# Decoding weights in the first batch's GEMM slots: the intermediate in PSUM, half of the low bits on GpSimd, two pieces ahead instead of four

## The chip, the core and the metric

The kernel runs on one core of one Trainium2 chip. The core has five engines that each work through their own instruction queue and meet only at semaphores: TensorE (PE in the profile, with PEld its weight loads), VectorE (DVE), ScalarE (ACT), GpSimd (POOL) and SyncE (SP), which here issues most of the DMAs. The metric is the device time of one execution in microseconds (us). Lower is better.

## The reference

Four batches, each in two stages: an mLSTM attention with gates (8 heads, 768 positions, head size 40), and a mixer that multiplies its output by two pairs of weight matrices.

```
for t in range(S):                                   # attention, per batch and head
    m_new = max(f[t] + m, i[t])
    C = exp(f[t] + m - m_new) * C + exp(i[t] - m_new) * outer(v[t], k[t])
    n = exp(f[t] + m - m_new) * n + exp(i[t] - m_new) * k[t]
    y[t] = sigmoid(o[t]) * (C @ q[t]) / max(|n . q[t]|, 1)
x = y as [4, 768, 320]
u = x + (relu(x.T @ w_tok1) @ w_tok2).T              # 768 -> 256 -> 768
out = u + relu(u @ w_ch1) @ w_ch2                    # 320 -> 1536 -> 320
```

The weights arrive as 64-bit floating-point numbers, so the kernel has to turn them into 32-bit ones itself before it can multiply by them.

## The kernel before

Attention works on chunks of 128 positions, a unit (b, c) being chunk c of batch b. The mixer of a batch consists of `a_part` and `a_end` (first pair, first product), `phase_b` (second product, added to x), `phase_t` (transposes of u, two blocks of 128 positions into one tile uT), and 18 GEMM slots. A slot (k, p) takes 256 positions k and 256 of the 1536 inner columns p: `gemm1` makes h in PSUM, ACT makes gh = relu(h) rounded, DVE makes gl = the remainder, and `gemm2`, which is issued one slot later, multiplies both by w_ch2. Every product is made of three matmuls, high by high, low by high and high by low half.

The first batch differs in that its weights are not there yet. They are decoded in 30 pieces of 128x384 numbers, 12 of them before the slots and the other 18 in slots 0 to 8, two in each; in order, two pieces of w_ch1 and two of w_ch2 in turn. The slots of this batch go (0,0), (1,0), (0,1), (1,1) and so on, so that two slots pass for each p. One piece goes through four engines:

- SP loads the raw 64-bit words into a tile wst (line 581).
- `dec_abs` (lines 587 to 598): ACT takes the upper word as a float, its absolute value times 2^-112, into a tile f (line 594), and puts the three top bits of the lower word into wst as an integer (line 595, "the low bits" below).
- `dec_ops` (lines 600 to 618): DVE shifts f left by three and ORs the low bits in (line 608, in place in f), then ORs the sign in (line 611) into the tile w.
- `dec_hi` (line 623): ACT rounds w to the high half c1h or c2h; `dec_low` (line 629): POOL subtracts for the low half c1l or c2l.

In the attention of the first batch (flag `early`) f lies in a PSUM bank of the pool ps_acc and is named pf in the profile. In the slots f lies in SBUF, is named wf, and f and w are the same tile.

PSUM has eight banks in four pools of two. The pool ps_s (tag "s") holds the attention's scores, and in the first batch's slots the outputs of `phase_t` and of `phase_b` 4 and 5, each bank being handed to the next tile of that tag in the order of the code.

The order on every engine is the order of the code. In one slot n of the first batch up to n = 10 that is: `dec_ops` (DVE), `gemm1` with gh and gl, `dec_hi`, `dec_low`, `dec_abs` for the next pieces, a piece of sigmoid or of the next batch's preparation, then in slots 3 and 4 `phase_b` 4 and 5 (the list `extra`), then `gemm2` of the slot before.

Of the kernel before, what the change touches and what calls it, by code (L numbers as in the profile page):

```python
# [7 lines left out]
F32 = mybir.dt.float32  # L8
F32R = mybir.dt.float32r
I32 = mybir.dt.int32  # L10
U16 = mybir.dt.uint16
BF16 = mybir.dt.bfloat16
AF = mybir.ActivationFunctionType
ALU = mybir.AluOpType
# [16 lines left out]
W_BIAS = 2.0 ** -112  # L31
# [3 lines left out]
def kernel(ctx: ExitStack, tc: tile.TileContext, gates, qk, q3, kv, og,  # L35
                            wt1, wt2, wc1, wc2, ident, bmask, out):
    nc = tc.nc
# [5 lines left out]
    ps_acc = ctx.enter_context(tc.tile_pool(name="ps_acc", bufs=2, space=PSUM))  # L43
    ps_s = ctx.enter_context(tc.tile_pool(name="ps_s", bufs=2, space=PSUM))
    ps_m = ctx.enter_context(tc.tile_pool(name="ps_m", bufs=2, space=PSUM))

    def f32(x):
        return x.bitcast(F32)
# [8 lines left out]
    wq = tc.alloc_tile_pool(name="wq", bufs=1, side="right")  # L57
# [46 lines left out]
    floor_b = wp.tile([128, 1], F32, name="floor_b")  # L104
# [24 lines left out]
    def cols_w(c0, c1):  # L129
        n = c1 - c0  # L130
        t = ps_m.tile([128, n, B * HP], F32, tag="m", name="gw")
        e = id_t[0:B * HP, 0:B * HP]
        for i in range(n):
            a, z = (c0 + i) * L, (c0 + i + 1) * L
            nc.tensor.matmul(t[:, i], b_t[:, a:z], e, start=True, stop=False)
            nc.tensor.matmul(t[:, i], phi[:, z - 1:z].to_broadcast([B * HP, 128]), e, start=False, stop=True)
        return t
# [427 lines left out]
    WP = 384  # L565
# [6 lines left out]
    staged, ready = {}, {}  # L572
    nxt = [0, 0, 0]
    his, lows, wx, early = [], [], [], [True]
# [12 lines left out]
    def dec_abs(n):  # L587
        while nxt[1] < min(n, len(pieces)):
            raw = staged[nxt[1]]
            if early[0]:  # L590
                f = ps_acc.tile([128, WP], F32, tag="acc", name="pf")
            else:
                f = wq.tile([128, WP], F32, tag="wf", name="wf", bufs=4)
            nc.scalar.activation(f, raw[:, :, 1].bitcast(F32), AF.Abs, scale=W_BIAS)  # L594
            nc.scalar.activation(raw[:, :, 0], raw.rearrange("p n t -> p (n t)").bitcast(U16).rearrange("p (n t) -> p n t", t=4)[:, :, 1],  # L595
                                 AF.Identity, scale=2.0 ** -13, bias=floor_b)
            ready[nxt[1]] = (f, wq.tile([128, WP], F32, tag="wf", name="wf", bufs=4) if early[0] else f)
            nxt[1] += 1

    def dec_ops(more, m=2):  # L600
# [19 lines left out]
    def dec_hi():  # L620
        while his:
            _, _, f, d, _, a = his.pop(0)
            nc.scalar.activation(d[0][:, a:a + WP], f, AF.Copy)
            lows.append((f, d, a))

    def dec_low():
        while lows:
            f, d, a = lows.pop(0)
            nc.gpsimd.tensor_tensor(d[1][:, a:a + WP], f, f32(d[0][:, a:a + WP]), ALU.subtract)
# [9 lines left out]
    def a_part(b, j, s):  # L639
        _, xh, xl = xs[(b, s)]  # L640
        if s == 0:
            pa[j] = ps_h.tile([128, DM], F32, tag="h", name="ps_a")
        a = slice(s * DT + j * 128, s * DT + (j + 1) * 128)
        t = [(w1[0][:, a], xh), (w1[1][:, a], xh), (w1[0][:, a], xl)]
        mm3(pa[j], t, s == 0, s == NC - 1)
# [43 lines left out]
    acc = {}  # L689
# [16 lines left out]
    def gemm2(b, k, p, gh, gl, half=None):  # L706
        if p == 0 and half != 1:
            pool = (ps_m, "m") if (b, k) == (0, 1) else (ps_acc, "acc")
            acc[k] = [pool[0].tile([128, DM], F32, tag=pool[1], name=f"acc{i}") for i in range(2)]
        for tt in range(2) if half is None else (half,):  # L710
            t = slice(tt * 128, (tt + 1) * 128)
            a = [slice((2 * p + j) * DM, (2 * p + j + 1) * DM) for j in range(2)]
            mm3(acc[k][tt], [(gh[:, j, t], c2[x][:, a[j]]) for j in range(2) for x in range(2)]
                + [(gl[:, j, t], c2[0][:, a[j]]) for j in range(2)], p == 0, p == NF // 2 - 1)
            if p == NF // 2 - 1:
                s = 2 * k + tt
                x = xs[(b, s)][0]
                nc.vector.tensor_tensor(x, acc[k][tt], x, ALU.add)
                nc.sync.dma_start(out=out[b, s * 128:(s + 1) * 128, :], in_=x)


    def step(g, n=1):
        for _ in range(n):
            next(g, None)
# [37 lines left out]
    t = cols_w(0, 1)  # L762
# [12 lines left out]
    step(g, 9)  # L775
    split(1, 2)
    dec_abs(2)
    warm(10)
    spread_split(u1)
    t = cols_w(1, NC - 1)  # L780
# [88 lines left out]
    for b in range(B):  # L869
        if b:  # L870
            for j in range(2):
                for s in range(NC - 1):
                    a_part(b, j, s)
        if b == 1:
            step(ag)
        if b:
            gemm2(*pend, half=0)
        for j in range(2):
            a_part(b, j, NC - 1)
            a_end(b, j)  # L880
        if b:
            gemm2(*pend, half=1)
            pend = None
            phase_b(b, 0)
            phase_b(b, 1)
            if b < B - 1:
                phase_b(b, 2)
                phase_t(b, 0, ss)
                phase_t(b, 1, ss)
                step(ag, 2)  # L890
                phase_b(b, 3)
            else:
                phase_t(b, 0, ss)
                phase_b(b, 2)
                phase_t(b, 1, ss)
                phase_b(b, 3)
                step(ag)
        if b:
            slots = [(k, p) for k in range(3) for p in range(6)]
        else:  # L900
            dec_hi()
            step(dg, 1)
            sp.release()
            wx += [tc.alloc_tile_pool(name="wx", bufs=1, side="right"), nxt[0]]
            dec_load(nxt[0] + 3)
            dec_hi()
            dec_low()
            pf = prep_first(units[NC], units[NC + 1])
            dec_abs(nxt[2] + 4)
            phase_b(b, 0)  # L910
            step(dg, 9)
            phase_b(b, 1)
            phase_t(b, 0, ss)
            phase_b(b, 2)
            phase_t(b, 1, ss)
            phase_b(b, 3)
            dec_hi()
            dec_low()
            slots = [(k, p) for p in range(6) for k in range(2)] + [(2, p) for p in range(6)]
        extra = []  # L920
        more = {1: [(phase_b, 4, ss)], 2: [(phase_t, 2, ss)], 4: [(phase_t, 3, ss)], 5: [(phase_b, 5)],
                9: [(phase_t, 4), (phase_t, 5, ss)]}
        for n, (k, p) in enumerate(slots):
            if b == 0 and n == 3:
                extra = [lambda: phase_b(0, 4, ss), lambda: phase_b(0, 5, ss)]
            if b == 0 and n == 1:
                gemm2(*pend)
                pend = None
            if b == 0 and n < 11:
                dg = dec_ops(9)  # L930
                step(dg, 4 if n == 0 else 9)
            g = gemm1(b, k, p)
            if b == 0 and n == 0:
                step(dg, 9)
            if b == 0:
                if n == 0:
                    phase_t(b, 2, ss)
                    phase_t(b, 3, ss)
                    warm(6, id_t.bitcast(BF16))
                if n == 11:  # L940
                    phase_t(0, 4, ss)
                    phase_t(0, 5, ss)
                    gemm2(*pend)
                    pend = None
                    wx[0].release()
                    wq.release()
                    xpool[1] = ctx.enter_context(tc.tile_pool(name="xp", bufs=1, side="right"))
                    step(ag)
                if n < 11:
                    dec_hi()  # L950
                    dec_low()
                    dec_abs(nxt[2] + 2)
                    if n < 6:
                        sigmoid(1, (n // 3,), slice(n % 3, n % 3 + 1))
                    if n in (0, 5, 7, 8, 9):
                        step(pf)
                elif n > 11:
                    o = STEPS0[n - 12]
                    step(ag, o[0])
                    gemm2(*pend, half=0)  # L960
                    step(ag, o[1])
                    gemm2(*pend, half=1)
                    pend = None
                    step(ag, o[2])
            else:
                for f, *a in more.get(n, ()):
                    f(b, *a)
                step(ag, STEPS[n])
            if extra:
                extra.pop(0)()  # L970
            if pend:
                gemm2(*pend)
            pend = (b, k, p) + g
# [56 lines left out]
```

## Time and profile before

| | us |
|---|---|
| median of 3 runs (lowest, highest) | 453.13 (451.94, 453.14) |
| the profiled execution | 453.32 |
| its span, first to last instruction | 451.5 |
| mean granted TensorE clock | 0.989 of full speed |

The span is 1.8 us shorter than the time of the same execution; what lies around it is launch and end. Times in the rows count from the span's start. The first batch's attention fills about 0 to 62 us, the steps before its slots 62 to 68.6, slots 0 to 11 from 68.6 to 117.6, and from there on the other batches' attention is interleaved with the slots.

A timeline row has the start, the duration, the engine, the line, the operation, the tiles as out<-in with their shapes, and how many instructions it sums; in brackets how long the engine had been idle and what ended it. A wait row has the engine and line, what it waited for, the sum, how often, and the longest. PEclk is the clock granted to TensorE in parts of full speed: 1.00 is 2.4 GHz and 0.50 is 1.2 GHz.

### The profile page before, as it was taken

The numbers are of one execution on the slowest core, as the hardware profiler recorded it, in microseconds if no ns is written. First come the engines' busy times: TensorE is split into PE (matmuls) and PEld (weight loads), VectorE is DVE, ScalarE is ACT, GpSimd is POOL, SyncE is SP. The second block draws the span as 40 slices with busy tenths as digits, with TensorE's granted clock in tenths as the row PEclk, the third lists the DMA queues.
The fourth block names the chain that finished last, engine by engine and source line by source line (L and its number), as shares of the span: only waits on it lengthen the run. The fifth ranks groups of instructions, "written<-read, shape, count | busy, mean of one in ns | idle before, by whom it ended". The sixth has DMA issues, their size and how long they took to land.

```text
span 451.5 us, 9377 instructions
## 1 busy us (share of the span) xinstructions
PE 434.0 (96%) x3717; PEld 413.8 (92%) x3718; DVE 304.9 (68%) x664; ACT 187.0 (41%) x429; POOL 126.1 (28%) x159
## 2 busy tenths in 40 slices
PE   6699989999999989999999999999999999999997
PEld 3478878999999989999999999999999999999996
DVE  6598968875567567879888578879887635232212
ACT  3437685988344462532341353441442212112111
POOL 4046642465045331034224212223314110000000
PEclk9899989999999989999999999999999999999999
DMA  8818875770276851313533621312631000000000
GB/s 223 277 42 265 247 232 194 233 225 19 97 217 198 242 181 63 132 43 95 165 111 120 205 70 50 134 47 78 176 105 43 1 2 29 1 1 29 1 30 29
DMA packets 24615, 52.55 MB, mean 116 GB/s; under 512 B 2556, under 2 KB 13364, under 8 KB 24572
## 3 DMA queue, kind: packets, MB, share of 16 engines
q1 hardware_dynamic: 24380, 51.78, 37.3%
q8 instruction: 29, 0.48, 0.5%
q10 hardware_dynamic: 192, 0.18, 0.1%
q14 instruction: 14, 0.11, 0.1%
HBM read 47.91 MB, written 4.04 MB: 115 GB/s over the span
## 4 chain that ended last, share of the span: by engine, by line
PE 77%; DVE 4%; ACT 2%; DMA 1%; issue 1%; POOL 1%; DVEq 0%; ACTq 0%; SPq 0%
PE ps_h L635 27%; PE acc L635 26%; PE ps_sc L280 4%; PE ps_a L635 4%; PE ps_b L635 4%; PE po L370 3%; PE po L396 2%; DVE wf L608 2%; PE pu L348 2%; PE po L375 2%; DMA wst<-in_wc_dram 1%; DVE wf L611 1%; PE po L340 1%; ACT wf L594 1%; ACT wst L595 1%
## 5 line engine op out<-in xcount | busy, mean ns | idle before, releaser
L635 PE MATMUL ps_h<-uT,c1h 128*128 128x256 f32 x720 | 140.3, 282 | 0.9 <-DVE uT L686 0.8
L702 ACT ACTIVATE gh<-ps_h 128x512 fp32r<-128x512 f32 x72 | 43.0, 597 | 180.1 <-PE ps_h L635 180.1
L635 PEld LDWEIGHTS ps_h<-uT,c1h 128*128 128x128 f32 x720 | 115.4, 188 | 2.0 <-DVE uT L686 1.0
L635 PE MATMUL ps_h<-uT,c1l 128*128 128x256 f32 x432 | 111.4, 280 | 0.0
L703 DVE SCALAR_TENSOR_TENSOR gl<-ps_h,gh 128x512 fp32r<-128x512 f32 x72 | 49.6, 689 | 82.4 <-ACT gh L702 82.1
L635 PE MATMUL acc<-c2h,gh 128*128 128x320 f32 x288 | 91.2, 324 | 0.0
L635 PE MATMUL acc<-c2l,gh 128*128 128x320 f32 x288 | 87.2, 311 | 0.0
L635 PEld LDWEIGHTS ps_h<-uT,c1l 128*128 128x128 f32 x432 | 81.4, 188 | 0.0
L635 PE MATMUL acc<-c2h,gl 128*128 128x320 f32 x288 | 66.4, 312 | 0.8 <-DVE gl L703 0.8
L635 PEld LDWEIGHTS acc<-c2h,gh 128*128 128x128 f32 x288 | 54.7, 190 | 1.3
L635 PEld LDWEIGHTS acc<-c2l,gh 128*128 128x128 f32 x288 | 54.8, 190 | 0.0
L635 PEld LDWEIGHTS acc<-c2h,gl 128*128 128x128 f32 x288 | 48.3, 189 | 1.9 <-DVE gl L703 1.8
L261 ACT ACTIVATE dd<-dd,bcol 128x128 f32<-128x128 f32 x144 | 45.8, 393 | 4.7 <-POOL dd L251 4.7
L415 POOL TENSOR_TENSOR sig<-sig,ht 128x320 f32<-128x320 f32 x18 | 14.8, 824 | 112.6 <-DVE ht L378 102.3
L290 DVE TENSOR_TENSOR dd<-ps_sc,dd 128x512 f32<-128x512 f32 x48 | 31.0, 681 | 3.0 <-PE ps_sc L280 2.9
L465 POOL TENSOR_TENSOR xl<-x,xh 128x320 fp32r<-128x320 f32 x18 | 15.8, 877 | 47.2 <-DVE xh L463 47.2
L280 PE MATMUL ps_sc<-raw 40*128 40x128 f32 x384 | 28.6, 285 | 0.0
L280 PEld LDWEIGHTS ps_sc<-raw 40*128 40x128 f32 x384 | 23.9, 187 | 3.7 <-issue 1.7
L396 PE MATMUL po<-kvt,dd 128*128 128x41 f32 (+1 forms) x192 | 23.6, 280 | 1.7 <-issue 1.7
L396 PEld LDWEIGHTS po<-kvt,dd 128*128 128x128 f32 x192 | 22.8, 194 | 1.9 <-issue 1.9
L251 POOL TENSOR_SCALAR_AFFINE_SELECT dd<-dd 128x1024 f32<-128x1024 f32 x18 | 22.9, 1273 | 3.7 <-DMA dd<-phi_d 1.9
L303 DVE TENSOR_TENSOR r<-dd 128x512 f32<-128x512 f32 x24 | 22.6, 979 | 0.0
(135 smaller groups left out, 760.6 us busy)
## 6 DMA issues: line engine op xcount, KB each, us to landing
dd<-phi_d SPq DMA_DIRECT2D x18, 512.0 KB
wst<-in_wc_dram SPq DMA_DIRECT2D x22, 384.0 KB
kvt<-in_kv_dram SPq DMA_DIRECT2D x24, 324.0 KB
raw<-in_qk_dram SPq DMA_DIRECT2D x48, 160.0 KB
sig<-in_og_dram SPq DMA_DIRECT2D x8, 480.0 KB
out_dram<-x SPq DMA_DIRECT2D x24, 160.0 KB
q3t<-in_q_dram SPq DMA_DIRECT2D x20, 180.0 KB
wst<-in_wt_dram SPq DMA_DIRECT2D x8, 384.0 KB
```

The lines of the kernel that those rows point to most:

```text
L251: nc.gpsimd.affine_select(dd, dd, pattern=[[0, H], [1, L]], compare_op=ALU.is_ge, fill=-1e30, base=0, channel_multiplier=-1)
L261: nc.scalar.activation(dd[:, h, :], dd[:, h, :], AF.Exp, bias=bcol[:, c, HP * b + h:HP * b + h + 1])
L280: nc.tensor.matmul(t["s"][hf][:, h, :], r[:, 1, h, :], r[:, 0, h, :], start=True, stop=True)
L290: nc.vector.tensor_tensor(dd, t["s"][hf], dd, ALU.mult)
L303: nc.vector.tensor_tensor(r[:, h], dd[:, h], top(dd)[:, h], ALU.subtract)
L370: nc.tensor.matmul(po[:, h - h0, 0:j1 - j0], p[i][:, ROW[h], :], w[:, h, j0:j1], start=h == h0 and i + j0 == 0, stop=c == 0 and h == h1 - ...
L396: nc.tensor.matmul(o, t["dd"][:, ROW[h], :], x, start=c == 0 and h == 0, stop=h == H - 1)
L415: nc.gpsimd.tensor_tensor(sg, sg, ht[:, :, 0:D], ALU.mult)
L465: nc.gpsimd.tensor_tensor(xl, x, f32(xh), ALU.subtract)
L635: nc.tensor.matmul(ps, a, m, start=(first and i == 0), stop=(last and i == n - 1))
L702: nc.scalar.activation(gh, ps, AF.Relu)
L703: nc.vector.scalar_tensor_tensor(gl, ps, 0.0, f32(gh), op0=ALU.max, op1=ALU.subtract)
```

## The change

Five edits in the decode of the slots. The tile f is a PSUM bank of ps_s in place of an SBUF tile, and w is always an SBUF tile of its own. Of the pieces in the slots every even one gets its low bits from GpSimd (a tensor_scalar, line 598 of the changed kernel), every odd one from ACT as before. The call of `dec_abs` ahead of slot 0 stands behind `phase_b` and `phase_t` in place of ahead of them, and it takes two pieces in place of four. `phase_b` 4 and 5 are issued ahead of `dec_abs` in slots 3 and 4 in place of behind the slot's other work. DMAs are issued in the same order.

```diff
     def dec_abs(n):
         while nxt[1] < min(n, len(pieces)):
             raw = staged[nxt[1]]
-            if early[0]:
-                f = ps_acc.tile([128, WP], F32, tag="acc", name="pf")
+            pool, tag = (ps_acc, "acc") if early[0] else (ps_s, "s")
+            f = pool.tile([128, WP], F32, tag=tag, name="pf")
+            nc.scalar.activation(f, raw[:, :, 1].bitcast(F32), AF.Abs, scale=W_BIAS)
+            low = raw[:, :, 0]
+            top16 = raw.rearrange("p n t -> p (n t)").bitcast(U16).rearrange("p (n t) -> p n t", t=4)[:, :, 1]
+            if early[0] or nxt[1] % 2:
+                nc.scalar.activation(low, top16, AF.Identity, scale=2.0 ** -13, bias=floor_b)
             else:
-                f = wq.tile([128, WP], F32, tag="wf", name="wf", bufs=4)
-            nc.scalar.activation(f, raw[:, :, 1].bitcast(F32), AF.Abs, scale=W_BIAS)
-            nc.scalar.activation(raw[:, :, 0], raw.rearrange("p n t -> p (n t)").bitcast(U16).rearrange("p (n t) -> p n t", t=4)[:, :, 1],
-                                 AF.Identity, scale=2.0 ** -13, bias=floor_b)
-            ready[nxt[1]] = (f, wq.tile([128, WP], F32, tag="wf", name="wf", bufs=4) if early[0] else f)
+                nc.gpsimd.tensor_scalar(low, top16, 2.0 ** -13, 2.0 ** -14 - 0.5, op0=ALU.mult, op1=ALU.add)
+            ready[nxt[1]] = (f, wq.tile([128, WP], F32, tag="wf", name="wf", bufs=4))
             nxt[1] += 1
@@ before slot 0
             pf = prep_first(units[NC], units[NC + 1])
-            dec_abs(nxt[2] + 4)
             phase_b(b, 0)
...
             dec_hi()
             dec_low()
+            dec_abs(nxt[2] + 2)
@@ in a slot
                     dec_hi()
                     dec_low()
+                    if extra:
+                        extra.pop(0)()
                     dec_abs(nxt[2] + 2)
...
-            if extra:
-                extra.pop(0)()
             if pend:
                 gemm2(*pend)
```

ACT's queue from the steps ahead of slot 0 to the first decode of slot 1, before (c2h and c1h are `dec_hi`, wf<-wst and wst<-wst the two halves of `dec_abs`, uT is `phase_t`):

```order
L623 ACTIVATE c2h<-wf 128x384 x2
L594 ACTIVATE wf<-wst 128x384
L595 ACTIVATE wst<-wst,floor_b 128x384
L594 ACTIVATE wf<-wst 128x384
L595 ACTIVATE wst<-wst,floor_b 128x384
L594 ACTIVATE wf<-wst 128x384
L595 ACTIVATE wst<-wst,floor_b 128x384
L594 ACTIVATE wf<-wst 128x384
L595 ACTIVATE wst<-wst,floor_b 128x384
L685 ACTIVATE uT<-ps_t 128x3x128 x2
L702 ACTIVATE gh<-ps_h_929 128x512
```

and of the changed kernel, whose line numbers are two higher from line 599 on:

```order
L625 ACTIVATE c2h<-wf 128x384 x2
L687 ACTIVATE uT<-ps_t 128x3x128 x2
L592 ACTIVATE pf<-wst 128x384 x2
L596 ACTIVATE wst<-wst,floor_b 128x384
L704 ACTIVATE gh<-ps_h_925 128x512
```

Eight decode instructions stood ahead of the uT copies; three now stand behind them.

POOL's queue through the low halves of slots 0 to 3 in the changed kernel; before, the L631 rows (L629 there) stood next to each other:

```order
L631 TENSOR_TENSOR c1l<-wf,c1h 128x384 x2
L598 TENSOR_SCALAR wst<-wst 128x384
L631 TENSOR_TENSOR c2l<-wf,c2h 128x384 x2
L598 TENSOR_SCALAR wst<-wst 128x384
L631 TENSOR_TENSOR c1l<-wf,c1h 128x384 x2
L598 TENSOR_SCALAR wst<-wst 128x384
L631 TENSOR_TENSOR c2l<-wf,c2h 128x384 x2
```

Each new instruction stands behind the two subtractions of the slot before the one whose piece it serves.

PE's queue in slot 3, with waits, before (ps_b is `phase_b` 4, acc the `gemm2` of slot 2):

```order
L635 MATMUL ps_h_1108<-uT,c1l 128x256
L635 MATMUL ps_b<-rh,w2h 128x320
L635 MATMUL ps_b<-rh,w2l 128x320
L635 MATMUL ps_b<-rh,w2h 128x320
L635 MATMUL ps_b<-rh,w2l 128x320
```

and now:

```order
L637 MATMUL ps_h_1116<-uT,c1l 128x256
L637 MATMUL ps_b<-rh,w2h 128x320 [waits DVE_49]
L637 MATMUL ps_b<-rh,w2l 128x320
L637 MATMUL ps_b<-rh,w2h 128x320
L637 MATMUL ps_b<-rh,w2l 128x320
```

The order is the same; the first matmul of `phase_b` 4 now waits for DVE, whose line 611 (613 now) of slot 3's first piece is the last reader of the bank it writes. That of `phase_b` 5 in slot 4 has the same new wait.

## Rows read from the trace of the kernel before

**Rows 1.** The page: busy time, share of span and instructions of each engine.
```profile
PE 434.0 (96%) x3717; PEld 413.8 (92%) x3718; DVE 304.9 (68%) x664; ACT 187.0 (41%) x429; POOL 126.1 (28%) x159
```

**Rows 2.** Waits of PE, 55 to 112: us in total, times, longest.
```profile
PE ps_a L635 <- ACT xh L446: 1.4, 1, 1.4
PE acc L635 <- DVE gl L703: 0.8, 3, 0.4
PE ps_h L635 <- DVE uT L686: 0.8, 1, 0.8
```

**Rows 3.** Timeline of DVE, slots 0 to 8: start, us, what, [idle before].
```profile
71.12 1.02 DVE L608 SCALAR_TENSOR_TENSOR wf<-wf,wst 128x384 int32<-128x384 int32 x2
72.06 1.02 DVE L611 SCALAR_TENSOR_TENSOR wf<-wst,wf 128x384 int32<-128x384 int32 x2
85.15 1.02 DVE L611 SCALAR_TENSOR_TENSOR wf<-wst,wf 128x384 int32<-128x384 int32 x2
87.83 1.53 DVE L608 SCALAR_TENSOR_TENSOR wf<-wf,wst 128x384 int32<-128x384 int32 x2 [0.37 <-ACT wst L595]
106.52 1.02 DVE L611 SCALAR_TENSOR_TENSOR wf<-wst,wf 128x384 int32<-128x384 int32 x2
```

**Rows 4.** Timeline of PE in the slots, and after its longest later wait.
```profile
82.45 0.30 PE L635 MATMUL ps_b<-rh,w2h 128*128 128x320 f32 x1
86.98 0.31 PE L635 MATMUL ps_b<-rh,w2h 128*128 128x320 f32 x1
108.20 0.56 PE L635 MATMUL acc<-c2h,gl 128*128 128x320 f32 x2 [0.20 <-DVE gl L703]
163.34 2.46 PE L396 MATMUL po<-kvt,dd 128*128 128x41 f32 x16 [1.74 <-issue]
```

**Rows 5.** Timeline of ACT between two decode steps.
```profile
85.74 1.00 ACT L623 ACTIVATE c2h<-wf 128x384 fp32r<-128x384 f32 x2 [0.31 <-DVE wf L611]
87.09 0.66 ACT L595 ACTIVATE wst<-wst,floor_b 128x384 int32<-128x384 uint16 x1
87.62 0.56 ACT L594 ACTIVATE wf<-wst 128x384 f32<-128x384 f32 x1
88.06 0.65 ACT L595 ACTIVATE wst<-wst,floor_b 128x384 int32<-128x384 uint16 x1
```

**Rows 6.** Timeline of POOL, the low halves of slots 0 and 3.
```profile
73.81 2.00 POOL L629 TENSOR_TENSOR c1l<-wf,c1h 128x384 fp32r<-128x384 f32 x2 [8.66 <-ACT c1h L623]
86.34 2.01 POOL L629 TENSOR_TENSOR c2l<-wf,c2h 128x384 fp32r<-128x384 f32 x2 [2.11 <-ACT c2h L623]
```

**Rows 7.** Waits of DVE, 68 to 112.
```profile
DVE wf L608 <- POOL c1l L629: 2.1, 2, 1.0
DVE wf L608 <- POOL c2l L629: 2.1, 2, 1.0
```

**Rows 8.** Timeline around the first slot, ACT and PE.
```profile
67.73 0.86 ACT L685 ACTIVATE uT<-ps_t 128x384 fp32r<-128x384 f32 x2
70.14 0.71 PE L635 MATMUL ps_h<-uT,c1h 128*128 128x256 f32 x3 [0.77 <-DVE uT L686]
```

**Rows 9.** Groups of POOL by form: busy, mean ns, idle before.
```profile
L629 POOL TENSOR_TENSOR c2l<-wf,c2h 128x384 fp32r<-128x384 f32 x10 | 10.0, 1023 | 12.0 <-ACT c2h L623 12.0
L102 POOL COPY sel<-id 128x360 bf16<-128x360 bf16 x1 | 0.5, 484 | 0.1
L92 POOL CAST late_b<-late 128x128 bf16<-128x128 f32 x1 | 0.3, 291 | 0.1
```

**Rows 10.** Timeline of DVE and POOL, attention stage: the intermediate pf in PSUM.
```profile
55.30 0.57 DVE L608 SCALAR_TENSOR_TENSOR pf<-pf,wst 128x384 int32<-128x384 int32 x1
54.86 1.04 POOL L629 TENSOR_TENSOR w2l<-wf,w2h 128x384 fp32r<-128x384 f32 x1
```

**Rows 11.** Windows: busy PE, PEld, DVE, ACT, POOL, then PEclk, DMA share, GB/s.
```profile
62.00:66.00 4.00, 3.86 (x15) 3.21 (x14) 2.50 (x7) 3.70 (x9) 1.99 (x2) 0.57 0.72 226
164.00:169.00 5.00, 5.00 (x27) 5.00 (x28) 2.83 (x8) 4.31 (x11) 1.91 (x3) 0.66 0.44 134
```

## The prediction

> **What bounds the kernel now.** I read the page first: PE is busy for 96% of the span [rows 1], so time is to be won or lost only where PE waits or runs at its lower clock. In PE's waits from the last attention unit of batch 0 to slot 10 the reader sees two small sums inside the changed stretch: 0.8 us for the transposed uT at slot 0 and 0.8 us, in three pieces, for the remainder gl in slots 6 to 8 [rows 2]. Then I followed what gl stands behind, DVE's timeline. In each slot DVE does the pair at line 608, the pair at line 611, then gl; the line-611 pairs begin at 72.06 in slot 0, 85.15 in slot 3, 106.52 in slot 8 [rows 3]. That is 34.46 us for eight rounds, 4.3 on average. DVE is far behind PE: slot 3's line-611 pair begins at 85.15, while PE has finished `gemm1` of slot 3 at 82.45 [rows 3, 4].
>
> The decode runs in a ring, here from slot 3 to slot 4. Line 611 begins at 85.15; ACT's rounding begins at 85.74, 0.59 later [rows 5]; POOL's subtractions begin at 86.34, 0.60 later, and take 2.01 [rows 6]; the ACT decode of the next pair is done at 88.06 + 0.65 = 88.71 [rows 5], yet DVE's line-608 pair, which began at 87.83 on the first piece, takes 1.53 in place of the 1.02 it takes when POOL is idle [rows 3]. It is held until POOL ends at 88.35. Waits of 4.2 us in total stand to POOL's name at this line [rows 7]. So the ring already closes on POOL's end, and PE begins to feel it in slot 6.
>
> **What each edit costs.** (1) `dec_abs` behind `phase_t`. Today ACT copies uT from 67.73, after eight decode instructions, and PE waits 0.77 at 70.14 for DVE's part [rows 8]. Without them the copies start as the transposes end; DVE's later work in that stretch moves forward by the same 0.8, so slot 0's line-611 pair begins near 71.3. PE gains little of it: its next work is `phase_t` 2, whose ps_s bank the line-611 instruction of slot 0's first piece must free first, 0.51 after 71.3 [rows 3]. That is about 71.9, where it starts today. I book nought for PE and minus 0.76 for the ring.
>
> (2) Low bits on POOL. ACT loses 87.62 - 87.09 = 0.53 per slot [rows 5], which the ring does not feel. POOL gets one instruction behind each pair of subtractions, and the first line 608 waits for its result. Its price P is shown by no row. From above, the subtraction of the same 384 elements, with two inputs, took 1.02; from below, a cast of 128 elements took 0.29. A one-input copy of 360 elements took 0.48, so 384 would take about 0.50 [rows 9]. It is the nearest, but its elements lie side by side and need no arithmetic, while here they are 8 bytes apart, with two operations and two conversions. I take 0.6.
>
> The Trainium skill (GPSIMD Engine Reference, section 7, Performance pitfalls for Q7 kernels) puts reads of up to 8 bytes step at about 1.9 cycles an element, and only wider steps at 2.9; at the 1.2 GHz of its section 1 that would be 384 x 1.9 / 1.2 = 0.61 us, an estimate from that page, before any start-up, and the sum below would be the same to 0.1. Its section 4.1 calls one-input work roughly line-rate, which at one element a cycle would be 0.32 and make the sum about 2 us smaller. No row here shows a strided read on POOL.
>
> (3) The intermediate in PSUM. Line 608 then runs beside POOL: in the attention stage, where f was in PSUM, it took 0.57 at 55.30 inside a subtraction that ran from 54.86 for 1.04 [rows 10]. So the hold of up to 0.5 per round goes, and the two line-608 instructions take 0.94 to the start of line 611 [rows 3]. But the round gains nothing from it, because DVE now waits for POOL by dependency, to the same POOL end and P beyond.
>
> The hand-over from POOL to DVE I take as 0.05, an estimate from the 0.08 between the end of the first line-611 instruction (85.15 + 0.51) and ACT's start. The new round: 0.59 + 0.60 + 2.01 + P + 0.05 + 0.94 = 4.19 + P, at P = 0.6 4.79, against 4.13 today from slot 3 to 4. Carried through: in slot 0 POOL's pair starts at 73.81 and takes 2.00 [rows 6], perhaps 0.15 later now; line 611 of slot 1 then begins at 73.96 + 2.00 + 0.6 + 0.05 + 0.94 = 77.55. Seven more rounds of 4.79 end at 111.1.
>
> (4) `phase_b` 4 in slot 3. Its bank is that of slot 3's first piece, so its first matmul waits for line 611 of slot 3, two rounds after 77.55, 87.1 + 0.55 = 87.7. PE is ready at about 82.45, as today [rows 4]. It waits about 5.2 us, with `gemm2` of slot 2 and `gemm1` of slot 4 queued behind it. Even with today's DVE times it would wait until 85.7, 3.2 us. What PE loses there it partly has back, since it then runs behind the ring and no longer waits in each slot. But from `phase_b` 4 to the end of `gemm1` in slot 4 PE needs 86.98 - 82.45 = 4.53 [rows 4], so slot 4's h is there at 92.2, and gh(4), 0.50 on ACT, stands ahead of that slot's rounding, which the ring would have wanted at 92.5. Rounding starts near 92.8: plus 0.3 on the ring. `phase_b` 5 then finds its bank nearly free.
>
> Sum on the ring: slot 8's line-611 pair begins at 111.1 + 0.3 = 111.4 against 106.52, plus 4.9. In slot 8 PE waits for gl both before and after [rows 4], so it passes on whole. Behind slot 8 nothing takes it back: the next batch's scores are issued on PE behind slot 11, and their loads wait on PE's and DVE's progress.
>
> (5) The clock. After PE's wait of 1.4 us at 59 to 61 [rows 2] the window 62 to 66 shows a granted clock of 0.57, most of it at 0.50, or 1.2 GHz; after the 1.74 before 163.34 [rows 4] the window 164 to 169 shows 0.66 [rows 11]. The loss is 4 x 0.43 = 1.7 and 5 x 0.34 = 1.7 us of work. A wait of 5.2 us is longer than both, and the work behind it up to gh(4) is on the ring; I book 1.5, since a part of the slow stretch may fall into the wait.
>
> Total: 4.9 + 1.5 = 6.4 on the profiled execution's 453.32, hence 459.7; the median stands 0.2 lower, which I ignore.
>
> **Rivals.** *The clock holds.* Then 453.3 + 4.9 = 458.2. For it: the 0.8 us waited at slot 0 lowered nothing that a row shows. Against it: both waits of 1.4 and more did.
>
> *POOL's instruction costs as much as a two-input one.* P = 1.02: seven rounds at 0.42 more and slot 1's, 3.4 on top, and `phase_b` 4 waits over 6 us; 463.1. Beyond it a second fall of the clock at `phase_b` 5 would add 1.5. From below, P = 0.29 takes 8 x 0.31 = 2.5 off: 457.2, and with the clock held 455.7.
>
> *Faster: the hold was the real ring.* If DVE's line 608 was held because both engines read SBUF, and POOL's low bits were ready by the time ACT has its own, a round would end on ACT, at 88.71 - 0.53 + 0.94 = 89.12, 3.97 after line 611, and PE's 0.8 at slot 0 and 0.8 at gl would go: 453.3 - 1.6 = 451.7. It decides where POOL's result is there by 88.18; but POOL's pair ends at 88.35, and the new instruction stands behind it. So it needs POOL's subtractions to get faster too, by (P + 0.17)/2 each; no row speaks for that.
>
> The Trainium skill (SBUF — State Buffer, section Who interferes with whom) says that a DVE instruction with two SBUF inputs contends with a GpSimd instruction that reads SBUF, one with a single SBUF input does not; rows 7 and 10 agree, and it is this page that would forecast the gain.
>
> *No change.* PE's 5.2 us would have to be won back in its later slots; only the 0.8 of rows 2 is there to be won, so it needs `phase_b` 4 to get its bank by about 84. 453.3.
>
> **How the numbers follow.** Stall, longer ring and lower clock 0.60 (459.7; its own range 457.2 to 463.1), clock holds 0.18, dear POOL instruction with a second fall 0.09 (464), no change 0.07, faster 0.06. A measurement tells about 0.3%, 1.4 us, from no change. Faster 0.06, same 0.07, slower 0.87. The range 455.7 to 464.0 takes in P from 0.29 to 1.02, the clock either way, and half of the dear case; left out are 0.07 + 0.06 + 0.05 = 0.18.
>
> **What would show it.** PE's timeline: idle ahead of `phase_b` 4 in slot 3, about 5 us, released by line 613 (611 before), then PEclk 0.50 for some us. DVE's waits at line 610 under the name of the new POOL instruction, and line-613 pairs 4.8 apart. The POOL row of line 598 near 0.6. uT's wait at slot 0 smaller. I am wrong if DVE's pairs come under 4.2 apart, if `phase_b` 4 waits under 2 us, or if the slots end less than 1.4 us later than today.

## The result, and the profile after

| | before | after |
|---|---|---|
| median of the timed executions, us | 452.53 (451.77 to 453.14) | 456.53 (456.20 to 458.32) |
| the profiled execution, us | 453.32 | 456.20 |
| its span, us | 451.5 | 454.4 |

The change makes the kernel slower: the ratio is 1.0104 (95% interval 1.0063 to 1.0145), or +4.0 us against the +6.4 forecast. The time lies within the forecast range. Lines from 599 on have numbers two higher than in the rows of before.

The page, beside [rows 1], shows that PE hardly changes; DVE and ACT are busy for 4.7 and 4.2 us less, and nine instructions went from ACT to POOL.

```profile
PE 434.1 (96%) x3717; PEld 413.5 (91%) x3718; DVE 300.2 (66%) x664; ACT 182.8 (40%) x420; POOL 129.4 (28%) x168
```

PE's waits from 55 to 116, beside [rows 2], in us in total, times and longest:

```profile
PE ps_b L637 <- DVE wf L613: 5.0, 1, 5.0
PE ps_t L684 <- DVE wf L613: 0.9, 1, 0.9
PE acc L637 <- DVE gl L705: 0.8, 1, 0.8
```

The new wait stands where it was expected, at `phase_b` 4. The wait for uT of [rows 2] is gone, and one of nearly the same length, for the ps_s bank of `phase_t`, has taken its place.

DVE's timeline, beside [rows 3], from slot 0 on (start, us, what, and in brackets how long DVE had been idle and what ended it):

```profile
69.67 1.01 DVE L613 SCALAR_TENSOR_TENSOR wf<-wst,pf 128x384 int32<-128x384 int32 x2
76.09 1.02 DVE L613 SCALAR_TENSOR_TENSOR wf<-wst,pf 128x384 int32<-128x384 int32 x2
84.66 1.03 DVE L610 SCALAR_TENSOR_TENSOR pf<-pf,wst 128x384 int32<-128x384 int32 x2 [2.17 <-POOL wst L598]
85.60 1.01 DVE L613 SCALAR_TENSOR_TENSOR wf<-wst,pf 128x384 int32<-128x384 int32 x2
90.37 1.01 DVE L613 SCALAR_TENSOR_TENSOR wf<-wst,pf 128x384 int32<-128x384 int32 x2
97.67 1.01 DVE L613 SCALAR_TENSOR_TENSOR wf<-wst,pf 128x384 int32<-128x384 int32 x2
112.01 1.01 DVE L613 SCALAR_TENSOR_TENSOR wf<-wst,pf 128x384 int32<-128x384 int32 x2
```

The line-613 pairs are those of slots 0, 1, 3, 4, 5 and 8. In slot 3 the line-610 pair takes 1.03 and no longer 1.53; before it, though, DVE now waits 2.17 for POOL's low bits. From slot 3 to slot 4 the line-613 pairs stand 90.37 - 85.60 = 4.77 apart. From slot 4 to 5 it is 7.30.

POOL's timeline, beside [rows 6], with the new line:

```profile
82.06 1.95 POOL L631 TENSOR_TENSOR c1l<-wf,c1h 128x384 fp32r<-128x384 f32 x2 [2.16 <-ACT c1h L625]
84.09 0.53 POOL L598 TENSOR_SCALAR wst<-wst 128x384 int32<-128x384 uint16 x1
```

The low bits end at 84.62, and DVE begins at 84.66. PE's timeline at the stall and in slot 8, beside [rows 4], and its longest wait in batch 1's attention:

```profile
86.20 0.64 PE L637 MATMUL ps_b<-rh,w2h 128*128 128x320 f32 x1 [5.01 <-DVE wf L613]
113.67 0.57 PE L637 MATMUL acc<-c2h,gl 128*128 128x320 f32 x2 [0.84 <-DVE gl L705]
167.62 2.08 PE L396 MATMUL po<-kvt,dd 128*128 128x41 f32 x16 [0.41 <-issue]
```

Slot 8's product with gl comes 113.67 - 108.20 = 5.47 later than in [rows 4], while the wait in batch 1 fell from 1.74 to 0.41. Behind the stall ACT has gh of slot 4 ahead of the rounding; its timeline:

```profile
92.99 0.60 ACT L704 ACTIVATE gh<-ps_h 128x512 fp32r<-128x512 f32 x1 [2.80 <-PE ps_h L637]
93.49 0.93 ACT L625 ACTIVATE c1h<-wf 128x384 fp32r<-128x384 f32 x2
```

The windows, beside [rows 11] (length; busy time of PE, PEld, DVE, ACT and POOL with their instructions; PEclk, DMA share, GB/s):

```profile
62.00:66.00 4.00, 3.68 (x22) 2.96 (x23) 3.20 (x9) 1.66 (x4) 2.51 (x3) 1.00 0.81 262
86.00:90.00 4.00, 3.80 (x14) 3.80 (x15) 2.50 (x7) 2.67 (x6) 2.53 (x3) 0.50 0.65 196
164.00:169.00 5.00, 4.59 (x44) 4.28 (x40) 4.24 (x9) 2.39 (x8) 2.76 (x3) 1.00 0.71 245
```

From 86 to 90, behind the stall, PE runs at 0.50, or 1.2 GHz. The two falls of [rows 11] aren't in this execution.

### The profile page after: what moved, and what is told of

Same layout as the page of the kernel before. It is cut to its first block, busy times and chain, and to the rows that moved or that the text cites. A ratio compares the mean times of both kernels' runs of the same rounds, so it can differ in the third digit from the quotient of the medians.

```text
span 454.4 us, 9384 instructions
## 1 busy us (share of the span) xinstructions
PE 434.1 (96%) x3717; PEld 413.5 (91%) x3718; DVE 300.2 (66%) x664; ACT 182.8 (40%) x420; POOL 129.4 (28%) x168
## 4 chain that ended last, share of the span: by engine, by line
PE 76%; issue 7%; DVE 6%; ACT 5%; POOL 4%; DMA 1%; SPq 0%; DVEq 0%; POOLq 0%; ACTq 0%
PE ps_h L637 26%; PE acc L637 26%; PE ps_sc L280 4%; PE ps_b L637 4%; PE ps_a L637 3%; PE po L370 3%; PE po L396 2%; PE pu L348 2%; PE po L375 2%; DVE pf L610 2%; DVE wf L613 2%; POOL c1l L631 1%; POOL c2l L631 1%; ACT wst L596 1%; ACT dd L258 1%
## 5 line engine op out<-in xcount | busy, mean ns | idle before, releaser
L610 DVE SCALAR_TENSOR_TENSOR pf<-pf,wst 128x384 int32<-128x384 int32 x30 | 15.9, 561 | 16.4 <-POOL wst L598 15.2
L251 POOL TENSOR_SCALAR_AFFINE_SELECT dd<-dd 128x1024 f32<-128x1024 f32 x18 | 21.5, 1194 | 4.1 <-DMA dd<-phi_d 4.0
```

Of the source, the lines that this page charges most:

```text
L251: nc.gpsimd.affine_select(dd, dd, pattern=[[0, H], [1, L]], compare_op=ALU.is_ge, fill=-1e30, base=0, channel_multiplier=-1)
L610: v.scalar_tensor_tensor(fi, fi, 3, raw[:, :, 0], op0=ALU.logical_shift_left, op1=ALU.bitwise_or)
```

## The experiments

The timed medians differ by little more than one kernel's own executions do, so the stretches of the profiles are read too. "Ahead" ends at the first matmul of `gemm1` in slot 0; "slots" runs from there to the first ps_sc matmul behind slot 11; "attention" runs from that to batch 1's first ps_a matmul; "po wait" is PE's longest wait in it. All are us; the ratio is to the kernel before, timed on the same chip.

| kernel | ahead | slots | attention | po wait | median | ratio (95%) |
|---|---|---|---|---|---|---|
| before, three profiles | 68.64, 67.57, 68.32 | 49.00, 50.36, 50.31 | 51.01, 52.06, 51.83 | 1.74, 2.08, 2.02 | 452.53 | 1 |
| after, three profiles | 67.18, 67.28, 66.50 | 55.92, 56.73, 56.37 | 48.28, 49.78, 51.83 | 0.41, 0.74, 1.59 | 456.53 | 1.0104 (1.0063 to 1.0145) |
| low bits first | 66.54 | 51.15 | 48.24 | 0.52 | 452.12 | 1.0008 (0.9970 to 1.0046) |
| late `phase_b` | 67.98 | 54.60 | 48.57 | 0.84 | 455.68 | 1.0074 (1.0041 to 1.0107) |
| both of these | 68.10 | 47.39 | 52.10 | 1.66 | 449.09 | 0.9947 (0.9905 to 0.9990) |
| all on ACT, late `phase_b` | 66.76 | 49.51 | 48.90 | 1.18 | 451.94 | 0.9983 (0.9948 to 1.0017) |
| all on ACT | 67.76 | 52.68 | 50.12 | 1.07 | 455.14 | 1.0062 (1.0029 to 1.0095) |
| before, `dec_abs` moved | 66.91 | 48.67 | 50.04 | 0.76 | 450.65 | 0.9955 (0.9924 to 0.9987) |
| before, POOL's low bits | 67.33 | 55.26 | 48.30 | 0.57 | 457.26 | 1.0104 (1.0067 to 1.0142) |
| filler in the stall | 67.88 | 54.12 | 52.25 | 1.77 | 455.74 | 1.0080 (1.0046 to 1.0114) |

Each edited kernel has one profile. That of "both of these" comes from an execution of 452.55 and that of the filler from one of 459.33, each over 3 us above its kernel's median.

**Low bits first.** In the changed kernel `dec_abs` goes ahead of `dec_low`, so that POOL makes the low bits before the subtractions:

```diff
                     dec_hi()
-                    dec_low()
                     if extra:
                         extra.pop(0)()
                     dec_abs(nxt[2] + 2)
+                    dec_low()
```

> The changed kernel, with the GpSimd low-bits instruction of a slot issued ahead of that slot's two subtractions in place of behind them; nothing else moves. Theory (two causes that cover for each other: the ring waits for GpSimd's new instruction because it stands behind the subtractions, and phase_b 4 waits for the ring because of its bank): line-613 pairs come under 4.2 us apart in place of 4.78, the wait ahead of phase_b 4 shrinks from 5.0 to about 2.5 us, and the time falls to 452.5 to 454.5. Rival 1 (the bank alone decides): the wait stays at 5 and the time at 456.5. Rival 2 (the dear GpSimd instruction alone decides, the bank wait only takes up slack): 452.0 or less.

The slots take 51.15, about 5 us less than in the changed kernel, and the stall becomes shorter. PE's wait:

```profile
PE ps_b L637 <- DVE wf L613: 2.0, 1, 2.0
```

POOL's instruction is the same, 0.54 to 0.57 in the slots; its place in the queue was the price. Most rounds are now 3.5 to 4.5 long, but the one behind the stall still takes 6.29. The median of 452.12 lies below the theory's 452.5 to 454.5 and so near rival 2's 452.0 that the time can't tell these two apart; the kernel with both edits does.

**Late `phase_b`.** In the changed kernel `phase_b` 4 and 5 move to slots 9 and 10, behind the ring:

```diff
-            if b == 0 and n == 3:
+            if b == 0 and n == 9:
                 extra = [lambda: phase_b(0, 4, ss), lambda: phase_b(0, 5, ss)]
```

> The changed kernel, with phase_b 4 and 5 issued in slots 9 and 10 in place of 3 and 4, when no weight piece uses the banks any more; GpSimd keeps its place. Theory (two causes): the 5.0 us wait and the fall of TensorE's clock behind it go, but PE waits about 1.1 us for gl in each of slots 2 to 7 in its place, since the decode round stays at 4.78; time 454.5 to 456, less than half of the loss comes back. Rival 1 (the bank alone): 452.5 or less, as before the change. Rival 2 (GpSimd alone): 456.5, no change.

PE's waits then hold 5.0 us again, in six pieces:

```profile
PE acc L637 <- DVE gl L705: 5.0, 6, 0.9
```

So with a ring of 4.77 the single stall was in large part the form in which PE met that ring; without it the wait is spread over the slots, and only about 1.7 us of the slots are won. The ratio moves from 1.0104 to 1.0074, less than the intervals can tell apart.

**Both.** The two edits above together:

> Both edits of the two kernels above: GpSimd's low bits ahead of the subtractions, and phase_b 4 and 5 in slots 9 and 10. Theory (two causes): neither the wait ahead of phase_b 4 nor waits for gl above 0.3 us are left, line-613 pairs under 3.9 apart, and the time is 1 to 2 us below that of the kernel before: 450.5 to 451.5. Rival 1: as with phase_b late alone, 452.5. Rival 2: as with low bits first alone, 452.

DVE's timeline and POOL's in the ring:

```profile
86.60 0.57 DVE L610 SCALAR_TENSOR_TENSOR pf<-pf,wst 128x384 int32<-128x384 int32 x1 [0.40 <-ACT wst L596]
87.07 1.01 DVE L613 SCALAR_TENSOR_TENSOR wf<-wst,pf 128x384 int32<-128x384 int32 x2
90.58 1.01 DVE L613 SCALAR_TENSOR_TENSOR wf<-wst,pf 128x384 int32<-128x384 int32 x2
```

```profile
84.74 2.00 POOL L631 TENSOR_TENSOR c2l<-wf,c2h 128x384 fp32r<-128x384 f32 x2 [0.85 <-ACT c2h L625]
86.83 0.54 POOL L598 TENSOR_SCALAR wst<-wst 128x384 int32<-128x384 uint16 x1
```

Now POOL has its low bits done before it begins the next subtractions, and the second piece's low bits on ACT close a round of 90.58 - 87.07 = 3.51. In the slots PE waits only at `phase_t`. This version is faster than both kernels, and by more than expected: 449.09 against 452.75 of before on the same chip. Its slots take 3.8 us less than with the low bits first alone and 7.2 less than with the late `phase_b` alone: each of the two causes had hidden a part of the other.

**All low bits on ACT, without the stall and with it.** In the changed kernel `if early[0] or nxt[1] % 2:` becomes `if True:`; in the first of the two with the late `phase_b` as well.

> The changed kernel with all low bits on ScalarE (nothing new on GpSimd) and phase_b 4 and 5 in slots 9 and 10. Theory: what is left of the change is the PSUM intermediate and two pieces ahead; DVE's line 610 no longer waits for GpSimd, but ScalarE's part of the round was as long (88.71 against GpSimd's 88.35 in the kernel before), so line-613 pairs come 4.0 to 4.1 apart, with waits of up to 0.4 for gl; time within 1 us of 452.5. Rival (the hold of line 608 by GpSimd was the round's true limit): pairs 3.7 apart or less, no waits for gl, 451 or less.

> The changed kernel with all low bits on ScalarE again; the PSUM intermediate, two pieces ahead, and phase_b 4 and 5 in slots 3 and 4 as changed. Theory (the bank alone costs a wait even with the short round): line-613 pairs 4.0 apart as in the run with phase_b late, a wait of about 3 us ahead of phase_b 4, mostly with a fall of the clock behind it, and a time 0.5 to 2 us above that run's 451.9, so 452.5 to 454. Rival (the wait needs the slow round): a wait under 1 us and 451.9.

Without the stall the line-613 pairs stand about 4.02 apart, and the waits for gl that I had thought possible don't come. With the early `phase_b` most pairs keep a distance of 4.0 to 4.5, but the round behind the stall takes 6.43, and the stall costs 3.2 us of the slots and 3.2 of the median, more than I had expected. PE's wait and the row of ACT behind it:

```profile
PE ps_b L637 <- DVE wf L613: 3.6, 1, 3.6
```

```profile
91.78 0.60 ACT L704 ACTIVATE gh<-ps_h 128x512 fp32r<-128x512 f32 x1 [2.69 <-PE ps_h L637]
```

ACT waits 2.69 for slot 4's `gemm1`, with the next round's rounding behind it: the stall lengthens the ring by itself, whoever makes the low bits.

**The moved `dec_abs` alone.** In the kernel before, with nothing else of the change:

```diff
             pf = prep_first(units[NC], units[NC + 1])
-            dec_abs(nxt[2] + 4)
...
             dec_low()
+            dec_abs(nxt[2] + 2)
```

> The kernel before, with one edit of the change alone: dec_abs behind phase_t and two pieces ahead in place of four. Theory: the 0.77 us wait for uT at slot 0 goes and nothing else moves by more than 0.3 us; time 0 to 1 us below the kernel before. Rival (four pieces ahead were needed): new waits of DVE for ScalarE in slots 1 and 2, and a time 1 us or more above.

It is faster than before, by more than expected. DVE's timeline ahead of slot 0, in the first profile of before:

```profile
68.24 0.42 DVE L686 TENSOR_TENSOR uT<-ps_t,uT 128x256 fp32r<-128x256 f32 x1 [1.40 <-ACT uT L685]
```

and here, ahead of slot 0 and in it:

```profile
65.54 0.42 DVE L686 TENSOR_TENSOR uT<-ps_t,uT 128x256 fp32r<-128x256 f32 x1 [0.23 <-ACT uT L685]
69.35 1.02 DVE L611 SCALAR_TENSOR_TENSOR wf<-wst,wf 128x384 int32<-128x384 int32 x2
```

DVE no longer waits 1.40 for ACT's half of the copy, but 0.23. Slot 0's line-611 pair begins 72.06 - 69.35 = 2.71 earlier than in [rows 3], 1.6 and 2.4 earlier than in the two repeats of before (below).

**POOL's low bits alone.** In the kernel before, with f still in SBUF:

```diff
-            nc.scalar.activation(raw[:, :, 0], ..., AF.Identity, scale=2.0 ** -13, bias=floor_b)
+            if early[0] or nxt[1] % 2:
+                nc.scalar.activation(low, top16, AF.Identity, scale=2.0 ** -13, bias=floor_b)
+            else:
+                nc.gpsimd.tensor_scalar(low, top16, 2.0 ** -13, 2.0 ** -14 - 0.5, op0=ALU.mult, op1=ALU.add)
```

> The kernel before, with one edit of the change alone: the low bits of every even piece on GpSimd, behind the subtractions; the intermediate stays in SBUF, phase_b has its own time. Theory (the place in GpSimd's queue lengthens the round): line-608 waits under the name of the new instruction, line-611 pairs 4.7 or more apart, waits of about 1 us for gl in slots 2 to 8, no wait ahead of phase_b 4, 455.5 to 457. Rival (only the bank costs): 452.5.

DVE's timeline (L612 and L600 are this kernel's numbers for line 608 and for the new instruction):

```profile
80.93 1.03 DVE L612 SCALAR_TENSOR_TENSOR wf<-wf,wst 128x384 int32<-128x384 int32 x2 [2.40 <-POOL wst L600]
85.74 1.03 DVE L612 SCALAR_TENSOR_TENSOR wf<-wf,wst 128x384 int32<-128x384 int32 x2 [2.23 <-POOL wst L600]
```

The round is 4.81, as with f in PSUM, and the pair takes 1.03 without PSUM, since it now starts when POOL has ended. This edit alone costs as much as the whole change in the median (457.26, four executions), and nearly as much in the slots (55.26). The waits for gl are fewer than expected: 3.9 us in four pieces.

**Filler in the stall.** In the changed kernel PE gets 30 matmuls whose result nobody reads, ahead of `phase_b` 4:

```diff
                     if extra:
+                        if n == 3:
+                            z = id_t.bitcast(BF16)
+                            t = ps_h.tile([128, 512], F32, tag="h", name="warm")
+                            for i in range(30):
+                                nc.tensor.matmul(t[:, 0:256], z[:, 0:128], z, start=i == 0, stop=i == 29)
                         extra.pop(0)()
```

> The changed kernel with 30 idle matmuls (128x256, about 0.11 us each) put between gemm1 of slot 3 and phase_b 4, in a ps_h bank, where PE waited 5.0 us; their output is not used. Theory (the clock's fall is a term of its own, since gh of slot 4 stands in the ring): the granted clock stays at 1.00 in that stretch, the round from slot 4 to 5 shrinks from 7.3 to about 5.3 us, and the time falls by 1.5 to 2.5 us, to 454 to 455. Rival (PE is behind the ring there, so its clock is free): the clock stays up and the time does not move, 456 to 457.

PE's timeline and a window over the same stretch:

```profile
83.26 3.44 PE L959 MATMUL warm<-id_t 128*128 128x256 bf16 x30 [1.38 <-DVE gl L705]
86.96 0.42 PE L637 MATMUL ps_b<-rh,w2h 128*128 128x320 f32 x1 [0.27 <-DVE wf L613]
```

```profile
84.00:90.00 6.00, 5.73 (x46) 5.21 (x45) 3.99 (x7) 4.16 (x10) 3.67 (x5) 1.00 0.62 210
```

DVE's line-613 pairs of slots 4 and 5:

```profile
91.15 1.01 DVE L613 SCALAR_TENSOR_TENSOR wf<-wst,pf 128x384 int32<-128x384 int32 x2
96.54 1.01 DVE L613 SCALAR_TENSOR_TENSOR wf<-wst,pf 128x384 int32<-128x384 int32 x2
```

The clock stays at 1.00, and these pairs stand 96.54 - 91.15 = 5.39 apart in place of 7.30; the slots take 2.2 less than the changed kernel's mean of 56.34. By the profile the lower clock is worth about 2 us. The timed median lies between the two expectations, and its interval overlaps that of the change, so the median alone doesn't show it. The single executions do more: six of the ten have a mean granted clock of 0.992 and took 454.0 to 456.0, all below the 456.2 of the changed kernel's fastest on another chip; the other four have 0.985 to 0.989 and took 457.6 to 459.3.

**Both kernels again.** Two more profiles of each, unchanged:

> The kernel before, unchanged, profiled once more. Theory (the clock falls, and the 1.74 us wait of batch 1's po matmul, vary from execution to execution): each of the two stretches 62 to 66 and 160 to 170 shows a fall in some executions and none in others, and the wait of the po matmul differs from 1.74 us by over 0.3 us; the slots, from their first gemm1 matmul to the first ps_sc matmul, take 49.0 us as before, within 0.3. Rival (they belong to the kernel): falls in both stretches, 62 to 66 and 164 to 169, and the wait at 1.74 us within 0.3, every time.

> The changed kernel, unchanged, profiled once more. Theory (the falls vary): the slots take 55.9 us within 0.3, the wait ahead of phase_b 4 stays at 5.0 us with a fall beside it, while the stretches 62 to 66 and 160 to 172 show falls in some executions, and the po wait differs from 0.41 us by over 0.3 us in one of two. Rival (the later end of the slots takes the po wait away): no fall in 62 to 66 and in 160 to 172, po wait 0.41 us within 0.3, in both executions.

> As the first repeat of the kernel before: by the theory at least one of the three profiles of this kernel lacks the fall at 62 to 66 or the one at 164 to 169, and the po wait takes other lengths than 1.74 us; by the rival all three agree.

> As the first repeat of the changed kernel: by the theory at least one of the three profiles of this kernel shows a fall at 62 to 66 or at 160 to 172, and the po wait takes other lengths than 0.41 us; by the rival all three agree. In each the slots take 55.9 us within 0.3.

These executions took 455.68 and 456.15 (before) and 458.70 and 460.15 (after). PE's timeline at the wait in batch 1, in the first and second repeat of before and then of after:

```profile
163.99 2.85 PE L396 MATMUL po<-kvt,dd 128*128 128x41 f32 x16 [2.08 <-issue]
```

```profile
164.61 2.71 PE L396 MATMUL po<-kvt,dd 128*128 128x41 f32 x16 [2.02 <-issue]
```

```profile
168.72 2.08 PE L396 MATMUL po<-kvt,dd 128*128 128x41 f32 x16 [0.74 <-issue]
```

```profile
168.43 3.13 PE L396 MATMUL po<-kvt,dd 128*128 128x41 f32 x16 [1.59 <-issue]
```

A window of the first repeat of before:

```profile
68.00:74.00 6.00, 5.24 (x30) 4.88 (x29) 5.36 (x14) 1.97 (x5) 0.00 (x0) 0.72 0.28 71
```

In the changed kernel both repeats show the wait of 5.0 ahead of `phase_b` 4 with a granted clock of 0.50 behind it, and the round from slot 4 to 5 takes 8.12 and 7.76. Both have a fall behind the po wait, at 170 to 176, and the first repeat one at 62 to 66, that its first profile lacks: the clock held there doesn't belong to the change. All three po waits of the changed kernel are shorter than the three of before, but they run from 0.41 to 1.59, so whether the shorter wait belongs to the change isn't shown. In the kernel before the theory is half borne out: both repeats lack the fall at 62 to 66 and have one at 68 to 74 instead, inside the slots, which is why these take 50.3 and not the 49.0 I expected, but the fall behind the po wait is in all three. The slots of the changed kernel, too, spread more than the 0.3 expected.

## Why the prediction was right, and where it was not

**The number.** The forecast of 459.7 is 3.2 above the measured 456.53, which lies below the main case's own range of 457.2 to 463.1. The whole range reaches down to 455.7 for a cheap POOL instruction with the clock held, and neither of these came true. What brought the time down is won ahead of the ring and in batch 1's attention, where the prediction booked nothing; that the range took it in is luck. The stall and the longer ring themselves came as forecast.

**Right: POOL's place closes the round.** The forecast had P = 0.6 and a round of 4.79; the new instruction took 0.53, with 0.08 ahead of it, and the round is 4.77. POOL's low bits alone gave nearly the same round (4.81) and the same ratio, and with them ahead of the subtractions the loss went (1.0008). The price of the instruction did not decide. The Trainium skill (GPSIMD Engine Reference, section 7) led to an estimate of 0.61 and its section 4.1 to 0.32; the measured 0.53 lies nearer the first, and below it.

**Right: PSUM gains the round nothing.** The hold at line 608 went, and the wait for POOL took its place. No run changes the bank alone. The nearest is "all on ACT, late `phase_b`", where the bank is in PSUM and POOL has nothing new: its rounds are 4.02 against 4.12 with the moved `dec_abs` alone, and its slots 49.51 against 48.67. What part PSUM has in the 3.51 of "both" wasn't tested.

**Right: the stall.** PE waited 5.01 against 5.2, for line 613 of slot 3.

**Too small: what the stall does behind it.** I booked 0.3 for gh(4) and 1.5 for the clock. The round from slot 4 to 5 takes 7.30 - 4.77 = 2.5 longer in the first profile, 3.4 and 3.0 longer in the repeats. With the filler, at full clock, it is 5.39: so 1.9 of the first profile's 2.5 go with the lower clock, and 0.6 are left for gh(4).

**The step that failed most: the moved `dec_abs`.** I wrote "I book nought for PE and minus 0.76 for the ring", read off PE's wait of 0.77 in [rows 8], and let slot 1's line-611 pair begin at 77.55. It began at 76.09, and at 76.19 and 75.40 in the repeats. DVE's own idle time ahead of the uT copy was the number to read: 1.4 before (2.0 and 2.2 in the repeats), 0.2 in the row of the moved `dec_abs` alone. In the mean of the three profiles each, slot 0's pair begins 2.1 earlier (69.48 against 71.59). So in slot 1 the ring is 1.7 us ahead of the forecast in the mean. Between slots 1 and 8 it loses 1.0 more than forecast: 36.34 in the mean, against 35.4 from 77.55 to 112.9, which is the forecast 111.4 with the 1.5 for the clock. The slots end 5.26 later (123.33 against 118.07), where I had 6.4; the rest of that difference is that the repeats of before end their own ring 0.3 and 1.0 later than the profile that I read.

**Failed: "Behind slot 8 nothing takes it back".** Batch 1's attention is 2.7 us shorter in the first pair of profiles and 1.7 in the means. By size the po wait and the fall of the clock behind it can make that difference: in the means the wait is 1.0 shorter (0.91 against 1.95), and the fall costs 1.7, 3.4 and 3.4 us of work in the three profiles of before (half of the time spent at 1.2 GHz), but 0, 1.7 and 3.4 in those of after, a part of it behind the attention. The wait hangs on a load: ACT waits for pq, and PE's po matmuls begin 3.91 or 4.27 to 4.28 behind the start of ACT's use of it in all six profiles. ACT's rows in the first profiles of before and after:

```profile
159.06 0.53 ACT L243 ACTIVATE pq<-pq 120x384 f32<-120x384 f32 x1 [4.29 <-DMA pq<-phi_d]
163.71 0.52 ACT L243 ACTIVATE pq<-pq 120x384 f32<-120x384 f32 x1 [2.19 <-DMA pq<-phi_d]
```

From the load's issue to ACT's use of it 10.1 to 10.5 us pass in the three profiles of before, and 9.2, 9.5 and 10.3 in those of after. I had treated the falls of one execution as fixed. Whether the change itself shortens that load somewhat, or three profiles each merely fell so, stays open: "filler in the stall" had its slots end nearly as late and shows the long wait (10.5 us, 1.77), while the moved `dec_abs` alone ends them early and shows a short one (0.76), and "both" ends them as early and shows a long one (1.66).

Put together from the means: 1.2 earlier into the slots, 6.45 longer in them, 1.7 back in the attention and 0.25 behind it, 3.3 us in the spans. The two medians differ by 4.0.

**The rivals.** The clock did not hold and POOL was not dear. "Faster: the hold was the real ring" fails as the prediction said it would, because the instruction stands behind the subtractions; with that undone and `phase_b` out of the way a round ends on ACT, at 3.51 where the rival had 3.97.

## What to carry to other kernels

An instruction given to another engine costs what stands ahead of it in that engine's queue, not its own duration: here 0.53 us of work behind 2 us of subtractions lengthened every round. One moved call took the loss away, and a second one, of `phase_b`, turned it into a gain. A bank handed to a ring must not be one that PE's next work needs before the ring has come round: with the short ring of all low bits on ACT that alone cost 3.2 us, with the fall of the clock behind it. And what a move makes earlier is read from the engine that feeds the ring, not from the wait on PE.

## What was not expected of the hardware

A wait of 1.4 us on PE, at 59 to 61 in every profile of before and after, was followed by a stretch at 1.2 GHz between 61 and 66 in the first profile of before and the first repeat of after, and by none at all before the stall in the other two of after. The repeats of before have theirs between 68 and 74 instead. The loss is the same 1.7 us or so each time ((1 - 0.72) x 6 in the window above), but where it falls, and whether, changed from execution to execution of one kernel.

The place between 68 and 74 has a nearer wait, which the moved `dec_abs` takes away: at slot 0 PE waits 1.41 and 1.57 us for the two halves of uT in the repeats of before and 1.38 with POOL's low bits alone, and these are the three profiles with a fall there. Of the ten profiles with the moved `dec_abs` none has a fall between 68 and 74, and five have none at all before slot 2. So that one call may spare a fall of the clock too; with one profile of most kernels this is a count, not a proof.

The falls show in the timed executions too: of the ten of "both", the six with a mean granted clock of 0.989 or 0.992 took 447.3 to 449.2, the four with 0.981 or 0.985 took 451.8 to 452.7. Within a single stretch, repeated profiles moved by 1.4 us in the slots and 3.6 in the attention, which is as much as most of these edits are worth.
